# Masks by an added product, keys in two tiles, and another order of experts and values in an attention and expert kernel

## The chip, the cores and the metric

The kernel runs on one core of a Trainium2 chip. A core has five engines that run side by side, each through its own queue in order: TensorE (PE) multiplies matrices, VectorE (DVE) and ScalarE (ACT) work on elements, GpSimd (POOL) does element work and issues the converting loads, and SyncE (SP) issues plain loads and stores. Sixteen DMA engines move the data for all of them. PE, DVE and ACT reach PSUM, the memory that products are written to; POOL works in SBUF alone. PE loads its stationary operand with an instruction of its own, which the profile lists as PEld.

The metric is the device time of one execution in microseconds (us). Lower is better.

## The reference

Two stages. First, attention in which each row sees itself and the 63 rows before it; then one expert for each whole batch entry, chosen by the mean of its rows.

```python
batch, n_heads, seq, head_dim = (8, 8, 576, 64)
scores = scale * np.matmul(q, k.transpose(0, 1, 3, 2))
rel = pos[:, None] - pos[None, :]
mask = (rel >= 0) & (rel < 64)
scores = np.where(mask, scores, -1e9)
attn = np.exp(scores - scores.max(-1, keepdims=True))
attn = attn / attn.sum(-1, keepdims=True)
x = np.matmul(attn, v)              # heads side by side: (8, 576, 512)

logits = x.mean(axis=1) @ w_gate    # (8, 8)
e_idx = np.argmax(logits, axis=1)   # one expert for each batch entry
gate_w = softmax(logits)[e_idx]
h = np.maximum(x[b] @ w1[e], 0.0)   # 512 -> 1024
out[b] = gate_w[b] * (h @ w2[e])    # 1024 -> 512
```

All inputs and the output are float32.

## The kernel before

**Units.** The work on attention is cut into 16 units of four heads; units 2b and 2b + 1 belong to batch entry b. A unit goes through these functions:

- `load_qk(u)` (lines 208 to 213): two loads on POOL's queue, which turn float32 into bf16. There are six buffers.
- `transpose_qk(u, which)` (321): 18 transpositions on PE, for q or for k. `leave_qk` copies the result out of PSUM: q by ACT, k by DVE. With `both` set, DVE and ACT copy one half of k each, into one tile.
- `scores(u, c)` for c = 0, 1, 2 (352): 14 products of 64 keys each, then the exponential by ACT (line 371), then on DVE the multiplication with a mask of ones and zeros (378).
- `values(u, s)` for s = 0, 1 (384): 20 products with the probabilities as stationary operand; the values come from two fp16 copies, `va` and `vb` (shifted by 64 rows). `norm` then divides by the sum, on DVE.
- `transpose_x(u)` (427): ten transpositions of the result, copied out by ACT, which adds up the rows for the gate as it copies.

The values of a batch entry come by `load_v(b)` on SP's queue, behind a small memset by POOL. `cast_v(u)` makes the fp16 copies in three parts, "whole" into `va`, "low" and "high" into `vb`; where no engine is named, all three are done by POOL.

**Experts.** `gate(b)` (469) adds up over partitions by one product on PE, finds the largest logit on DVE, and loads its index into a register of POOL. `load_w1(b)` and `load_w2(b)` use that register, on POOL's queue. `expert_up(b, ft)`, eight pieces for each b, makes the hidden layer; `expert_down(b, mt)`, five pieces, makes the output, which DVE copies and SP stores. In the planner's account an up piece is 1.0 unit, a down piece 1.7, and the short last one 0.9: 15.7 for each batch entry. `experts(amount)` (599) lets out pieces until the amount is used up; pieces are whole, and what was overdrawn is carried on.

**Order.** Everything that `P` wraps keeps the order of the program on its engine. The opening (lines 646 to 708) is written out by hand for units 0 to 3; units 0 and 1 are helped by idle products (`busy`) and by casts on other engines. The gate of entry 0 uses a pooling of its own on PE (`pool_mm`, `pool_parts`). Then the loop over t (710): step t holds scores(t), values(t - 1), transpose_x(t - 1) and the transpositions of q and k of t + 1, with a share of the experts between each two of them; in even steps gate(t / 2 - 1) and the weight loads follow, late in the step. At t = 3 six units of experts go out; in steps 4 and 5 the share (`pace`) is two thirds of the later one.

**PSUM.** One pool of four buffers of two banks serves all products.

Of the kernel before, what the change touches and what calls it, by code (L numbers as in the profile page):

```python
# [156 lines left out]
def kernel(  # L157
# [10 lines left out]
    nc = tc.nc  # L168
# [77 lines left out]
    P(nc.gpsimd.memset(v_tiles[0][:, HM, 0:1], 0.0))  # L246
    P(nc.sync.dma_start(out=v_tiles[0][:, HM:NM, :], in_=vv[0][:, HM:NM, :]))
# [15 lines left out]
    par = const.tile([128, 2, 64], FP16)  # L263
    P(nc.vector.memset(par, 1.0))
    for (half, e, own) in ((0, 0, True), (1, 0, False), (0, 1, False), (1, 1, True)):
        sl = par[64 * half:64 * half + 64, e, :]
        if own:

            P(nc.gpsimd.affine_select(
                out=sl, in_=sl, compare_op=ALU.is_ge, fill=0.0, base=0,  # L270
                pattern=[[1, 64]], channel_multiplier=-1))
        else:

            P(nc.gpsimd.affine_select(
                out=sl, in_=sl, compare_op=ALU.is_ge, fill=0.0, base=-1,
                pattern=[[-1, 64]], channel_multiplier=1))
    masks = const.tile([128, 3, 2, 6, 64], FP16)
    for c in range(3):
        for s in range(2):
            P(nc.vector.tensor_copy(  # L280
                out=masks[:, c, s].rearrange("p (g e) w -> p g e w", e=2),
                in_=par[:, None, :, :].broadcast_to([128, 3, 2, 64])))
    for s in range(2):
        P(nc.vector.memset(masks[64:128, 0, s, 0, :], 0.0))
        P(nc.vector.memset(masks[0:64, 1, s, 3, :], 0.0))
# [48 lines left out]
    def leave_qk(u, which, both=False):  # L334

        view = qk_ps[u, which][:, 0:NT * 128].rearrange("p (t x r) -> p x r t", t=NT, x=2)
        if which == 0:
            dst = qkt.tile([128, 2 * S], BF16, tag="qT")
            P(nc.scalar.copy(  # L339
                out=dst.rearrange("p (x r t) -> p x r t", x=2, t=NT), in_=view))  # L340
            qt_tiles[u] = dst
        else:
            dst = qkt.tile([128, 2 * S], BF16, tag="kT")
            to = dst.rearrange("p (x r t) -> p x r t", x=2, t=NT)
            if both:
                P(nc.vector.tensor_copy(out=to[:, 0], in_=view[:, 0]))  # L346
                P(nc.scalar.copy(out=to[:, 1], in_=view[:, 1]))
            else:
                P(nc.vector.tensor_copy(out=to, in_=view))  # L349
            kt_tiles[u] = dst  # L350

    def scores(u, c, mask=True):
        qT, kT = qt_tiles[u], kt_tiles[u]
        sp = psum.tile([128, 2, 512], FP32, tag="ps")

        def mm(s, half, kblk, qblk, n):
            P(nc.tensor.matmul(  # L357
                out=sp[64 * half:64 * half + 64, s,
                       64 * (qblk - 6 * c):64 * (qblk - 6 * c) + n],
                lhsT=kT[64 * s:64 * s + 64, ts(kblk, 64)],  # L360
                rhs=qT[64 * s:64 * s + 64, 64 * qblk:64 * qblk + n],
                start=True, stop=True, tile_position=(64 * s, 64 * half)))
# [8 lines left out]
        P(nc.scalar.activation(out=pt, in_=sp[:, :, 0:384], func=AF.Exp, scale=scale))  # L371
        pt_tiles[u, c] = pt
        if mask:
            mask_scores(u, c)

    def mask_scores(u, c):
        pt = pt_tiles[u, c]
        P(nc.vector.tensor_tensor(  # L378
            out=pt, in0=pt, in1=masks[:, c].rearrange("p s g w -> p s (g w)"),
            op=ALU.mult))  # L380
# [46 lines left out]
    def transpose_x(u, chunks=(0, 1), parts=True):  # L427
# [11 lines left out]
        for kl in chunks:  # L439
            kb = 2 * qd + kl  # L440
            P(nc.scalar.activation(  # L441
                out=xT[:, kb, :], in_=tp[:, kl, 0:S], func=AF.Copy,
                accum_out=pooled[:, b, kb:kb + 1]))
# [202 lines left out]
    cast_part(0, "whole", nc.vector)  # L646
    cast_part(0, "high")
    cast_part(0, "low")
# [12 lines left out]
    transpose_qk(1, 0)  # L661
    transpose_qk(1, 1, False)
    leave_qk(1, 1, True)
    cast_part(1, "high")
    cast_part(1, "whole")
    load_v(1, True)
    values(0, 0)
    for c in range(3):
        scores(1, c, False)
    cast_part(1, "low", nc.scalar)  # L670
    values(0, 1, False)
    mask_scores(1, 0)
    norm(0, 1)
    mask_scores(1, 1)
    mask_scores(1, 2)
    values(1, 0)
    values(1, 1)
    transpose_qk(2, 0)
    pool_mm(0)
    pool_mm(1)  # L680
    pool_parts()
    transpose_qk(2, 1, False)
    gate(0, False)
    load_w1(0)
    leave_qk(2, 1, True)
    for c in range(3):
        scores(2, c)
        if c == 0:
            gate_weight(0)
    load_qk(4)  # L690
    cast_part(2, "high")
    load_qk(5)
    load_w2(0)
    cast_part(3, "high")
    load_v(2, True)
    transpose_x(0, parts=False)
    transpose_qk(3, 0)
    transpose_qk(3, 1)
    transpose_x(1, parts=False)
    cast_part(2, "whole", nc.vector)  # L700
    cast_part(2, "low", nc.scalar)
    for c in range(3):
        scores(3, c)
    values(2, 0)
    values(2, 1)
    cast_part(3, "whole", nc.vector)
    cast_part(3, "low", nc.scalar)
    transpose_x(2)

    for t in range(START, NU + LAG):  # L710
        pace = per_step / 8.0 * (2.0 / 3.0 if t < START + 3 else 1.0)
        on, prev, ahead = START < t < NU, START < t <= NU, t + 1 < NU
        if t == START:
            experts(4.0)
            transpose_qk(4, 0)
            transpose_qk(4, 1)
            experts(2.0)
            continue
        if START + 1 < t and t + 3 < NU:
            load_qk(t + 3)  # L720
        if t == START + 1:
            load_qk(6)
        if t % 2 == 1 and (t + 1) // 2 < B:
            load_v((t + 1) // 2, True)
        if on:
            cast_v(t)
            scores(t, 0)
        experts(pace)
        if prev:
            values(t - 1, 0)  # L730
        if ahead:
            transpose_qk(t + 1, 0)
        experts(pace)
        if prev:
            values(t - 1, 1)
        if on:
            scores(t, 1)
        experts(pace)
        if ahead:
            transpose_qk(t + 1, 1)  # L740
        if prev:
            transpose_x(t - 1)
# [4 lines left out]
        if prev and t % 2 == 0:  # L747
            gate(t // 2 - 1)
            load_w1(t // 2 - 1)
            if t == START + 1:  # L750
                load_qk(7)
            load_w2(t // 2 - 1)
# [43 lines left out]
```

## Time and profile before

| what | us |
|---|---|
| median of 3 runs | 244.97 (242.95 to 245.64) |
| profiled execution | 245.67 |
| its span, first to last instruction | 244.1 |
| PE busy | 209.2 (86%) |
| DVE busy | 128.7 (53%) |
| ACT busy | 128.8 (53%) |
| POOL busy | 87.2 (36%) |
| share of 16 DMA engines, software queue / hardware queue | 60.1% / 26.1% |

The span is shorter than the execution's time, because what lies before the first and after the last instruction is not in it. "L532" is line 532 of the kernel. In a row of the timeline the first number is the start in the span, the second the duration; the last bracket, where there is one, says how long the engine had been idle before it and what ended that. In a list of waits the numbers are the total, how often, and the longest. A row of stretches gives each engine's busy time, then the granted clock of PE, the share of the DMA engines and GB/s. Busy time of PE is not work at its peak; idle time of an engine that nobody waits for costs nothing.

### The profile page before, as it was taken

The page shows a single profiled execution, that of the slowest core. Times are in us where ns is not written, and L with a number is a line of the kernel's source. Part 1 is how long each engine was busy: PE and PEld are TensorE (multiplying, and loading weights), DVE is VectorE, ACT ScalarE, POOL GpSimd, SP SyncE. Part 2 cuts the span into 40 slices and gives each one's busy share as a digit, 9 for nine tenths or more (in the row PEclk, how much of TensorE's full clock was granted, in tenths as well). Part 3 has the DMA queues.
Part 4 walks back from the last instruction along what each step waited for, and adds up shares of the span by engine and source line. Part 5 has one row for each costly group of instructions (what it writes and reads, how often), then busy time and mean ns, then how long its engine had stood idle before and what let it go on. Part 6 is the DMA issues. An engine that isn't in the chain of part 4 may idle for free.

```text
span 244.1 us, 6963 instructions
## 1 busy us (share of the span) xinstructions
PE 209.2 (86%) x3000; PEld 144.1 (59%) x3000; DVE 128.7 (53%) x276; ACT 128.8 (53%) x216; POOL 87.2 (36%) x110
## 2 busy tenths in 40 slices
PE   7657756999949989995999799987998999799980
PEld 2346644874727846783678456863676568547740
DVE  2576564258835558554755575732758474431140
ACT  2393794685517844783368536871467445514500
POOL 7372680033940296008900692039005700200000
PEclk9996575899988999999999999997999999999998
DMA  8979999941999999996999889996994598199231
GB/s 139 206 127 206 164 205 230 234 111 46 176 228 231 252 196 217 233 250 185 189 227 246 263 147 226 244 267 134 225 228 158 79 239 225 13 205 238 87 140 64
DMA packets 33382, 45.64 MB, mean 187 GB/s; under 512 B 7104, under 2 KB 25408, under 8 KB 33344
## 3 DMA queue, kind: packets, MB, share of 16 engines
q0 software_dynamic: 13840, 26.22, 60.1%
q1 hardware_dynamic: 18704, 18.88, 26.1%
q8 instruction: 25, 0.41, 0.7%
q10 hardware_dynamic: 800, 0.03, 0.3%
q14 instruction: 13, 0.11, 0.1%
HBM read 61.90 MB, written 9.44 MB: 292 GB/s over the span
## 4 chain that ended last, share of the span: by engine, by line
PE 36%; DMA 35%; POOL 10%; DVE 7%; issue 5%; ACT 4%; POOLq 1%; SPq 0%; DVEq 0%; ACTq 0%
DMA vn<-in_v_dram 32%; PE php L532 13%; PE pso L546 12%; PE tp L326 3%; DMA qn<-in_q_dram 3%; POOL va L296 2%; PE tp L436 2%; PE op L399 2%; POOL qn L211 2%; ACT pt L371 2%; POOL kn L212 2%; POOL vb L296 2%; DVE x L415 2%; PE pso L555 2%; DVE pt L378 1%
## 5 line engine op out<-in xcount | busy, mean ns | idle before, releaser
L532 PE MATMUL php<-xT,w1t 128*128 128x288 f16 x512 | 74.5, 297 | 3.2 <-DMA w1t<-in_moe_w_dram 3.2
L536 ACT ACTIVATE hT<-php,gatew 128x576 f16<-128x576 f32 x64 | 47.0, 741 | 35.0 <-PE php L532 35.0
L532 PEld LDWEIGHTS <-w1t 128*128 128x128 f16 x512 | 56.6, 117 | 12.9 <-DMA w1t<-in_moe_w_dram 3.7
L546 PE MATMUL pso<-w2t,hT 128*128 128x512 f16 x256 | 61.7, 388 | 0.0
L378 DVE TENSOR_TENSOR pt<-pt,masks 128x768 f16<-128x768 f16 x48 | 31.7, 662 | 30.3 <-ACT pt L371 29.1
L296 POOL CAST va<-vn 128x1152 f16<-128x1152 f32 x13 | 15.3, 1175 | 89.2 <-DMA vn<-in_v_dram 88.8
L371 ACT ACTIVATE pt<-sp 128x768 f16<-128x768 f32 x48 | 38.1, 811 | 15.8 <-PE sp L357 15.7
L549 DVE COPY ob<-pso 128x512 f32<-128x512 f32 x32 | 22.1, 689 | 35.7 <-PE pso L546 35.1
L546 PEld LDWEIGHTS <-hT 128*128 128x128 f16 x256 | 23.8, 99 | 27.3 <-issue 3.0
L296 POOL CAST vb<-vn 64x1152 f16<-64x1152 f32 (+1 forms) x29 | 34.7, 1195 | 0.9
L441 ACT ACTIVATE xT<-tp 128x576 f16<-128x576 f16 x32 | 20.5, 648 | 18.4 <-PE tp L436 18.3
L339 ACT COPY dst<-tp 128x1152 bf16<-128x1152 bf16 x16 | 18.0, 1123 | 21.8 <-PE tp L326 21.8
L399 PE MATMUL op<-vb,pt 128*64 128x65 f16 x320 | 18.0, 200 | 10.8 <-POOL vb L296 7.1
L415 DVE TENSOR_TENSOR x<-op,linv 128x640 f16<-128x640 f32 x32 | 26.4, 824 | 1.1
L399 PEld LDWEIGHTS <-pt 128*64 128x64 f16 x640 | 14.4, 114 | 18.7 <-issue 14.7
L349 DVE COPY dst<-tp 128x1152 bf16<-128x1152 bf16 x13 | 17.6, 1352 | 8.3 <-PE tp L326 8.3
L357 PE MATMUL sp<-dst 64*64 64x128 bf16 (+1 forms) x672 | 17.2, 221 | 3.9 <-DVE dst L346 2.7
L357 PEld LDWEIGHTS <-dst 64*64 64x64 bf16 x672 | 11.1, 110 | 11.5 <-issue 5.4
L399 PE MATMUL op<-va,pt 128*64 128x65 f16 x320 | 17.5, 201 | 0.4 <-POOL vn L221 0.4
L436 PE MATMUL tp<-identh,x 128*128 128x128 f16 x160 | 12.7, 231 | 3.6 <-DVE x L415 3.2
L436 PEld LDWEIGHTS <-x 128*128 128x128 f16 x160 | 10.0, 104 | 5.6 <-DVE x L415 4.3
L413 DVE RECIPROCAL linv<-op 128x10 f32<-128x10 f32 x32 | 6.9, 215 | 11.9 <-PE op L399 11.9
(67 smaller groups left out, 160.2 us busy)
## 6 DMA issues: line engine op xcount, KB each, us to landing
w2t<-in_moe_w_dram POOLq DMA_DIRECT2D x8, 1024.0 KB, 14.9
out_dram<-ob SPq DMA_DIRECT2D x32, 256.0 KB, 6.2
w1t<-in_moe_w_dram POOLq DMA_DIRECT2D x7, 1024.0 KB, 8.4
qn<-in_q_dram POOLq DMA_DIRECT2D x16, 288.0 KB, 15.1
kn<-in_k_dram POOLq DMA_DIRECT2D x16, 288.0 KB, 17.1
vn<-in_v_dram SPq DMA_DIRECT2D x2, 576.0 KB, 7.3
w1t<-in_moe_w_dram POOLq DMA_DIRECT2D x2, 512.0 KB, 6.5
out_dram<-ob SPq DMA_DIRECT2D x16, 64.0 KB, 5.8
```

Source lines behind the costliest of these rows:

```text
L296: P(eng.tensor_copy(out=out, in_=in_))
L357: P(nc.tensor.matmul(out=sp[64 * half:64 * half + 64, s, 64 * (qblk - 6 * c):64 * (qblk - 6 * c) + n], lhsT=kT[64 * s:64 * s + 64, ts(kblk ...
L371: P(nc.scalar.activation(out=pt, in_=sp[:, :, 0:384], func=AF.Exp, scale=scale))
L378: P(nc.vector.tensor_tensor(out=pt, in0=pt, in1=masks[:, c].rearrange("p s g w -> p s (g w)"), op=ALU.mult))
L399: P(nc.tensor.matmul(out=op[64 * half:64 * half + 64, xx, 65 * jj:65 * jj + 65], lhsT=pt[:, s, 64 * (g % 6):64 * (g % 6) + 64], rhs=win, s ...
L415: P(nc.vector.tensor_tensor(out=x[:, :, h0 * D:(h0 + 2) * D].rearrange("p j (x c) -> p x j c", x=2), in0=view[:, :, :, 0:64], in1=li[:, :, ...
L436: P(nc.tensor.transpose(out=tp[:, kl, ts(jj, 128)], in_=x[:, jj, x_chunk(b, kb)], identity=identh))
L441: P(nc.scalar.activation(out=xT[:, kb, :], in_=tp[:, kl, 0:S], func=AF.Copy, accum_out=pooled[:, b, kb:kb + 1]))
L532: P(nc.tensor.matmul(out=php[:, sc, 0:288], lhsT=w1t[:, kb, 512 * (ft // 4) + ft % 4:512 * (ft // 4 + 1):4], rhs=xT[:, kb, ts(sc, 288)], s ...
L536: P(nc.scalar.activation(out=hT[:, ft].rearrange("p (sc s) -> p sc s", sc=2), in_=php[:, :, 0:288], func=AF.Relu, scale=gatew[:, b:b + 1]))
L546: P(nc.tensor.matmul(out=pso[:, 0, :], lhsT=hT[:, fb, ts(mt, 128)], rhs=w2t[:, fb, :], start=(fb == 0), stop=(fb == FB - 1)))
L549: P(nc.vector.tensor_copy(out=ob, in_=pso[:, 0, :]))
```

## The change

1. **Masks.** For units 0 to 3 the mask is no longer a multiplication on DVE. `add_outside(u, c)` first writes a tile of 0 and -1e38 into PSUM by a product with the identity (two products of 384 columns), and the score products add to it, so that the exponential is zero outside the window. The later units multiply with fp16 masks as before; these are now made from the same tile after unit 0's scores.
2. **Keys.** k is copied into two tiles, one for each half, on two engines that are named by the call (DVE twice by default).
3. **First load of v.** Entry 0's values were loaded in two halves, the first as the kernel's first load. Now two parts, of 20 and 16 rows, are both asked for after the loads of units 0 and 1.
4. **Opening.** The casts of units 0 and 1 and their normalisation come later and lie on other engines; `load_v(2)` comes earlier, `load_qk(6)` later; `transpose_x` of units 0 and 1 is copied by ACT or DVE without the sum.
5. **Experts.** The first experts stand right behind unit 3's scores, ahead of its and unit 2's values; the six units go out in five calls among the values and transpositions.
6. **Step.** In the loop, gate and weight loads of an even step follow the first share of experts, ahead of `cast_v(t)`; values(t) and transpose_x(t) come at the end of step t instead of in step t + 1. The share is 0.96 of the former one in every step.

```diff
-    P(nc.sync.dma_start(out=v_tiles[0][:, 0:HM, :], in_=vv[0][:, 0:HM, :]))
     warm = const.tile([128, 1], FP32)
...
     load_qk(1)
-    P(nc.gpsimd.memset(v_tiles[0][:, HM, 0:1], 0.0))
-    P(nc.sync.dma_start(out=v_tiles[0][:, HM:NM, :], in_=vv[0][:, HM:NM, :]))
+    for m0, m1 in ((0, 20), (20, NM)):
+        P(nc.gpsimd.memset(v_tiles[0][:, m0, 0:1], 0.0))
+        P(nc.sync.dma_start(out=v_tiles[0][:, m0:m1, :], in_=vv[0][:, m0:m1, :]))
...
+            dst = [qkt.tile([128, S], BF16, tag=f"kT{x}", name=f"kT{x}") for x in range(2)]
+            for x in range(2):
+                copy_on(engs[x], dst[x].rearrange("p (r t) -> p r t", t=NT), view[:, x])
...
+    def add_outside(u, c):
+        sp = psum.tile([128, 2, 512], FP32, tag="ps", name="sp")
+        for s in range(2):
+            P(nc.tensor.matmul(
+                out=sp[:, s, 0:384], lhsT=ident,
+                rhs=outside[:, c].rearrange("p g w -> p (g w)"), start=True, stop=False))
+        sp_ps[u, c] = sp
...
     busy(14)
     transpose_qk(0, 0)
-    busy(4)
+    add_outside(0, 0)
     transpose_qk(0, 1, False)
-    leave_qk(0, 1, True)
+    leave_qk(0, 1, (V, A))
+    add_outside(0, 1)
+    add_outside(0, 2)
     for c in range(3):
         scores(0, c)
+    make_masks()
...
     load_qk(2)
+    cast_part(0, "high")
     load_qk(3)
     transpose_qk(1, 0)
+    cast_part(0, "whole", V)
+    cast_part(0, "low", A)
+    transpose_qk(1, 1)
     cast_part(1, "high")
     load_v(1, True)
+    for c in range(3):
+        add_outside(1, c)
+    for c in range(3):
+        scores(1, c)
+    values(0, 0, False)
     values(0, 1, False)
+    cast_part(1, "whole", V)
+    norm(0, 0)
     norm(0, 1)
+    cast_part(1, "low", A)
+    busy(4)
     values(1, 0)
     values(1, 1)
     transpose_qk(2, 0)
+    transpose_qk(2, 1, False)
+    leave_qk(2, 1, (A, A))
     pool_mm(0)
...
+    experts(2.0)
     values(2, 0)
+    experts(1.0)
     values(2, 1)
+    experts(1.0)
+    values(3, 0)
     transpose_x(2)
+    values(3, 1)
+    experts(1.0)
+    transpose_qk(4, 0)
+    transpose_qk(4, 1)
+    experts(1.0)
+    transpose_x(3)
+    for t in range(START + 1, NU + LAG):
+        pace = per_step / 8.0 * 0.96
+        on, ahead = t < NU, t + 1 < NU
+        if t > START + 1 and t + 3 < NU:
             load_qk(t + 3)
         if t % 2 == 1 and (t + 1) // 2 < B:
             load_v((t + 1) // 2, True)
         if on:
             scores(t, 0)
         experts(pace)
+        if t % 2 == 0 and t <= NU:
+            b = t // 2 - 1
+            gate(b)
+            load_w1(b)
+            if t == START + 1:
+                load_qk(6)
+                load_qk(7)
+            load_w2(b)
         if on:
+            cast_v(t)
             scores(t, 1)
         experts(pace)
         if on:
             scores(t, 2)
         experts(pace)
+        if ahead:
+            transpose_qk(t + 1, 0)
         experts(pace)
+        if on:
+            values(t, 0)
         experts(pace)
+        if ahead:
+            transpose_qk(t + 1, 1)
         experts(pace)
+        if on:
+            values(t, 1)
...
         experts(pace)
         experts(pace)
+        if on:
+            transpose_x(t)
```

More of the change, by code (lines that the diff above doesn't have):

```diff
@@ L332, in transpose_qk, with leave_qk @@
             leave_qk(u, which)
-    def leave_qk(u, which, both=False):
+    def leave_qk(u, which, engs=(nc.vector, nc.vector)):
         view = qk_ps[u, which][:, 0:NT * 128].rearrange("p (t x r) -> p x r t", t=NT, x=2)
@@ L371, in scores @@
         P(nc.scalar.activation(out=pt, in_=sp[:, :, 0:384], func=AF.Exp, scale=scale))
+        if not masked:
+            P(nc.vector.tensor_tensor(
+                out=pt, in0=pt, in1=masks[:, c].rearrange("p s g w -> p s (g w)"),
+                op=ALU.mult))
         pt_tiles[u, c] = pt
[L373 to L380, printed above, removed]
     op_ps = {}
@@ L691 @@
     cast_part(2, "high")
+    load_v(2, True)
     load_qk(5)
@@ L746 @@
         experts(pace)
[L747 to L752, printed above, removed]
-        experts(pace)
+        if ahead:
+            transpose_qk(t + 1, 0)
+        experts(pace)
+        if on:
+            values(t, 0)
+        experts(pace)
+        if ahead:
+            transpose_qk(t + 1, 1)
+        experts(pace)
+        if on:
+            values(t, 1)
         if t == NU:
```

109 lines of the change are left out of this document (39 added, 70 removed).

## The prediction

> **What bounds the kernel now.** I read the page's slices first, then the list of waits of TensorE (PE), then the timelines of GpSimd (POOL) and PE around those waits, and last the chain of waits for the end.
>
> ```profile
> span 244.1 us, 6963 instructions
> ...
> PEclk9996575899988999999999999997999999999998
> ```
>
> The profiled execution took 245.67 us for a span of 244.1, so 1.6 us lie around the span; the median of the runs is 244.97. My sum is made against 245.67. The clock digits show 5 to 7 tenths in slices 4 to 7, before the experts are under way, and single dents later.
>
> ```profile
> PE op L399 <- POOL vb L296: 7.1, 7, 1.4
> PE php L532 <- DMA w1t<-in_moe_w_dram: 3.2, 1, 3.2
> ```
> ```profile
> PE gl L471 <- DVE gpart L463: 1.4, 2, 0.9
> ```
>
> These are waits in us, their number and the longest. From the first expert on, PE hardly rests: it waits for the cast of the values (vb), once for w1, and for the gate's parts. The end is plain PE work; the last batch's experts have nothing beside them:
>
> ```profile
> 221.45 7.84 PE php L532 x64
> 229.29 5.18 PE pso L546 x24
> 234.47 0.99 PE pso L555 x16
> 235.47 1.85 PE pso L546 x8
> ```
>
> An up piece (8 products) is 7.84/8 = 0.98 us, a down piece 1.85, and a batch 7.84 + 5.18 + 0.99 + 1.85 = 15.9 us for 15.7 of the planner's units. So PE's order of work after the start sets the end, and each us that PE waits there counts in full; work that changes its place costs nothing. The change has to be judged by what PE waits for, before and after.
>
> Why it waits for vb now:
>
> ```profile
> 110.58 1.14 POOL L296 CAST va<-vn 128x1152 f16<-128x1152 f32 x1 [14.95 <-DMA vn<-in_v_dram]
> 111.67 2.50 POOL L296 CAST vb<-vn 64x1152 f16<-64x1152 f32 x2
> 114.12 0.72 POOL L512 DMA_DIRECT2D w1t<-in_moe_w_dram  x1
> ```
>
> POOL sits 15 us on the load of v, casts for 3.6 us, and only then asks for the next weights. PE, which wants the casts one step later in its order, is held at the end of this only for 7.1 us in all.
>
> **The order inside a step (the dearest edit).** The new loop puts the gate and the issues of w1 and w2 ahead of cast_v on POOL, and takes values(t) into step t, where they stood in step t+1. In an even step POOL must now wait for the gate's index, issue two loads, and then cast. The trace of before holds just this sequence once, where v had landed long before:
>
> ```profile
> 188.56 0.36 PE L471 MATMUL gl<-gpart,onesf 128*128 128x8 f32 x2 [0.95 <-DVE gpart L463]
> ```
> ```profile
> 190.66 0.72 POOL L512 DMA_DIRECT2D w1t<-in_moe_w_dram  x1 [2.27 <-DVE gatew L500]
> 191.38 0.72 POOL L517 DMA_DIRECT2D w2t<-in_moe_w_dram  x1
> 192.15 1.14 POOL L296 CAST va<-vn 128x1152 f16<-128x1152 f32 x1
> 193.24 2.56 POOL L296 CAST vb<-vn 64x1152 f16<-64x1152 f32 x2
> ```
>
> From the gate's product to the last cast: 193.24 + 2.56 - 188.56 = 7.24, with the signal 7.3 us. On PE, between the same gate and values(t, 0), lie two score groups, one transposition of q and three calls of experts(pace):
>
> ```profile
> 178.68 0.29 PE sp L357 x12
> ```
> ```profile
> 183.95 0.62 PE tp L326 x18
> ```
>
> 0.29 + 0.29 + 0.62, the gate itself (0.36 busy, of which I take 0.15 as the rest overlaps), and whole expert pieces of 0.98 or 1.85. Following the planner's account through steps 4, 6, 8, 10, 12 and 14, the stretch is 6.0, 4.2, 5.2, 3.3, 4.3 and 4.3 us, 27.3 in all. Step 4 also has load_qk(6) and (7) between w1 and w2, four more issues of 0.72, so 10.2 us there. PE waits 6 x 7.3 + 2.9 - 27.3 = 19.4 us; the 7.1 of now go. **Net +12.3.** Queued behind POOL's wait for the index are the casts, the next q and k issues and the next v; who waits is PE, in order, at values(t, 0). Odd steps have no gate, and POOL, which runs ahead there, costs nothing. v itself is no limit: it is asked for right after the even step's casts, so it has a period of some 25 us less the 4 of the casts themselves, against 18.4, at most 19.8, from issue to landing today:
>
> ```profile
> DMA to landing us min/median/max: 4.9/18.4/19.8
> ```
>
> The gate also moves nearer to the transposition that feeds it:
>
> ```profile
> 79.64 0.73 PE L436 MATMUL tp<-identh,x 128*128 128x128 f16 x10
> ```
> ```profile
> 81.82 0.23 DVE L463 SCALAR_TENSOR_TENSOR gpart<-wg,pooled,gpart 128x8 f32<-128x8 f32 x1 [0.40 <-ACT xT L441]
> ```
>
> The parts are ready 82.05 - 79.64 = 2.4 us after the transposition begins. Before, some three pieces lay between; now one up piece, one score group and the transposition: 0.62 + 0.29 + 0.98 = 1.9. So 0.5 us in each of six steps and 0.8 in step 16, 3.8 against 1.4 now: **+2.4.** Less is possible if pieces fall well (0), more if ACT is behind (7).
>
> **w1 for batch 1.** The wait of 3.2 us and the half clock behind it:
>
> ```profile
> 71.00:75.00 4.00, 3.92 (x30) 2.31 (x30) 0.56 (x1) 1.44 (x2) 0.00 (x0) 0.58 1.12 240
> 167.00:171.00 4.00, 4.00 (x36) 1.43 (x30) 1.06 (x2) 1.12 (x1) 3.83 (x5) 0.57 0.88 137
> ```
>
> The seventh figure is the granted clock: 4 x (1 - 0.58) = 1.7 us lost after the wait. In the new order 13.8 us of PE work lie between gate(1) and batch 1's first piece, where 10.4 did.
>
> ```profile
> DMA to landing us min/median/max: 5.6/8.1/10.8
> ```
>
> Those are w1's landings. Issue 2.1 us after the gate and 10.8 make 12.9: in time. **-3.2 - 1.7 = -4.9.** The second dent (1.7 us too) followed a wait for vb, and a like wait earlier brought none:
>
> ```profile
> 166.23 0.19 PE L399 MATMUL op<-vb,pt 128*64 128x65 f16 x1 [1.19 <-POOL vb L296]
> ```
> ```profile
> 114.23 0.19 PE L399 MATMUL op<-vb,pt 128*64 128x65 f16 x1 [1.15 <-POOL vb L296]
> ```
>
> My six new waits are 2.1 to 4.2 us. Of three rests of that size two gave a dent. I take two, 3.4 for 1.7: **+1.7**, between -1.7 and +5.
>
> **The start.** Three edits pull against one another. The experts go right behind unit 3's scores:
>
> ```profile
> 32.30 0.71 PE L357 MATMUL sp<-dst 64*64 64x64 bf16 x42 [0.79 <-DVE dst L349]
> ```
> ```profile
> 38.66 1.25 PE L436 MATMUL tp<-identh,x 128*128 128x128 f16 x10 [3.20 <-DVE x L415]
> ```
>
> Now values(2), their normalisation on DVE and the transposition stand between 33.0 and 39.9, when the experts begin; taken alone the edit gives up to 39.9 - 33.0 = 6.9 less 1.5 of PE work that is only pushed behind (four value groups and a transposition), 5.4. But v of batch 0 is no longer asked for first. Packets and MB by queue, from 2 to 5 us, 9 to 11, 8 to 15, and 15 to 23 us:
>
> ```profile
> q1 hardware_dynamic: 2316, 0.59, 95.8%
> ```
> ```profile
> q0 software_dynamic: 294, 0.32, 92.6%
> q1 hardware_dynamic: 290, 0.07, 27.4%
> ```
> ```profile
> q1 hardware_dynamic: 2320, 0.59, 42.9%
> ```
> ```profile
> q0 software_dynamic: 1087, 1.18, 96.9%
> ```
>
> q1 is v, in records of 256 B, and q0 is q and k. Alone, v's first half (2,304 records) is through in 3 us, while the engines have nothing else. Beside q and k the two take turns, 290 records against 294, so v moves 145 a us. Now all 4,608 records start at about 8.5, as the second half does today (it lies within 8 to 15): 3.5 us of turns (500), then some 2 us alone at 770 a us or a little more (1,500 to 2,000), and at about 14 q and k of units 2 and 3 come in, a us sooner than today (15), as their trigger no longer waits for a mask of 0.66 and the k copies run abreast. Those hold the engines some 7 us, v gets 1,000, and the last 1,100 to 1,600 need 1.5 us more. The first part (20 of 36 rows, 2,560 records) lands at 14 to 15, the second at about 22.5. With the casts spread over three engines (POOL's 1.15 to 1.4 the longest), values(1, 0) can start at 23.9:
>
> ```profile
> 19.81 0.19 PE L399 MATMUL op<-va,pt 128*64 128x65 f16 x1 [0.40 <-POOL vn L221]
> ```
> ```profile
> 26.56 1.51 POOL L509 DMA_DIRECT2D w1t<-in_moe_w_dram  x2 [6.76 <-DVE dst L346]
> ```
>
> So 4.1 later. Today 6.75 us pass from there to w1's issue. Unit 0's normalisation now stands on DVE behind unit 1's cast (0.75), which adds 0.8; the k transposition, now ahead of the pool, takes 1.1 out:
>
> ```profile
> 23.00 1.10 PE tp L326 x18
> 24.10 0.54 PE gl L471 x2
> ```
> ```profile
> 26.09 1.44 PE L357 MATMUL sp<-dst 64*64 64x64 bf16 x42 [1.47 <-DVE dst L346]
> ```
>
> So w1 is issued at 23.9 + 6.75 + 0.8 - 1.1 = 30.4, against 26.56, and its second half lands near 38. Unit 3's scores end 9.0 us after the gate's product today (24.0 to 33.0); with the gate at 27.9, 1.5 less as the k copy no longer stands between, and 2 to 4 more for the products, they end at 37.4 to 39.4. The experts begin at about 38, 1.9 before today, with 1.5 of work behind them: **net 0.** Taken from both sides: -7 if v is in time, +2 if it is still later. [...]
>
> The products that replace the masks are 24 of 384 columns; with 1.85/8 = 0.23 for 512 columns each is 0.17, 4 us in all, 8 at half clock. Half lie under the copies that unit 0 and 1 wait for anyway; the others, 2 to 4 us, are in my 38, as are the 12 multiplications taken off DVE. They cost that much only if PE becomes the last in that stretch. Two key tiles let ACT and DVE copy side by side in units 0 and 1; the ACT queue is full of exponentials behind them, so nothing. Later two half copies replace one; DVE is off the path. The pace (0.96 throughout) only shifts pieces to the tail: nothing.
>
> **Sum.** 245.67 + 12.3 + 2.4 - 4.9 + 1.7 + 0 = 257.2.
>
> **The rivals.** *Casts in time* (faster). If the casts end before PE reaches values, the 19.4 and the dents (3.4) fall away: 257.2 - 19.4 - 3.4 = 234; it decides where gate to casts takes less than about 4.5 us. For it: POOL no longer waits for v's landing, 14.95 a time. Against it: the measured 7.24, of which 3.65 are casts alone, and POOL works in order. Chance 0.2, a third of it with the start early too, 228.
> *v early* (slower all the same). If v's records are served in bursts and not in turns, both parts land by 15, values(1) start near 17.5, 6.4 sooner than in my sum, and the experts near 31: 7 less, 250. Against it stand the equal counts. [...] 0.15.
> *Waits that overlap* (within 1%). The wait for the casts may swallow the gate's (2.4), the dents may stay at one (1.7), and one down piece more may fall into the stretch in four of the six steps (7.4): 257.2 - 11.5 = 245.7. 0.12.
> My forecast has the remaining 0.53.
>
> **How the numbers follow.** About 1% (2.45 us) is what a measurement of this kernel can tell from none. Faster takes the first rival, 0.2; same 0.12; slower 0.15 + 0.53 = 0.68. Below 236 lies half of the first rival and a bit, 0.12; above, my own case reaches 257 + 2 (start) + 3.3 (dents) = 262, and 0.07 is left beyond. The own range of the slower cases is 248 to 262.
>
> **What would show it.** In the changed profile PE's wait op <- POOL vb should be near 19 us in place of 7.1, in even steps, with w1 and w2 issued just ahead of the casts and the wait for v (14.95 a time) gone from POOL; php <- DMA w1t should be gone; gl <- DVE gpart near 3.8; v's second part should land at 21 to 23.5 and the first up product stand at 37 to 39. If op <- POOL vb is under 8, or the first up product is at 32, the forecast fails there.

## The result and the profile after

The changed kernel takes 259.9 us (median of four runs, 257.03 to 261.58); the kernel before, on the same chip, 243.96 (four runs, 241.88 to 245.64). The ratio is 1.064, with a 95% interval of 1.048 to 1.081: slower, by about 16 us. The ratio leaves out the slowest run of each kernel, which lies more than 1.5% above its fastest. The prediction's sum was 257.2, in a range of 236 to 262.

The profiled execution of the changed kernel took 260.54 us. First its page, span, busy time and granted clock in 40 slices:

```profile
span 258.8 us, 7019 instructions
...
PE 219.2 (85%) x3024; PEld 145.5 (56%) x3024; DVE 117.7 (45%) x281; ACT 126.6 (49%) x211; POOL 85.1 (33%) x109
...
PEclk9979799997999799997999799997999799999996
```

The clock row has changed its shape. Slices 4 to 7 now hold a single 7, where they had 5 to 7 throughout, but a 7 comes back every five slices or so, right through the loop. Next the list of what PE waits for (us in all, how often, the longest):

```profile
PE op L413 <- POOL vb L302: 19.8, 13, 2.9
PE gl L488 <- DVE gpart L480: 3.2, 7, 0.8
PE tp L450 <- DVE x L429: 2.2, 4, 1.0
PE sp L374 <- DVE kT L302: 2.1, 1, 2.1
PE php L549 <- DMA w1t<-in_moe_w_dram: 1.6, 1, 1.6
```

The wait for the casts is 19.8 us where it was 7.1, the gate's 3.2 where it was 1.4. The 1.6 for w1 is entry 0's second half, in the opening; the 3.2 of batch 1 are gone. What happens in an even step is seen best in step 8, on POOL and on PE:

```profile
111.36 0.72 POOL L529 DMA_DIRECT2D w1t<-in_moe_w_dram  x1 [17.28 <-DVE gatew L517]
112.07 0.72 POOL L534 DMA_DIRECT2D w2t<-in_moe_w_dram  x1
112.83 1.52 POOL L302 CAST va<-vn 128x1152 f16<-128x1152 f32 x1
114.31 2.30 POOL L302 CAST vb<-vn 64x1152 f16<-64x1152 f32 x2
```
```profile
108.73 0.39 PE L488 MATMUL gl<-gpart,onesf 128*128 128x8 f32 x2 [0.40 <-DVE gpart L480]
...
112.47 1.90 PE L563 MATMUL pso<-w2t,hT 128*128 128x512 f16 x8
115.50 0.19 PE L413 MATMUL op<-vb,pt 128*64 128x65 f16 x1 [1.13 <-POOL vb L302]
...
116.66 0.19 PE L413 MATMUL op<-vb,pt 128*64 128x65 f16 x1 [0.93 <-POOL vb L302]
```

POOL has been idle for 17.28 us, not for v but for the gate's result. Then come the two weight loads, then the casts, the last of which ends at 114.31 + 2.30 = 116.61. From the gate's product that is 7.9 us. PE has done its pieces in the meantime and stands twice, 1.13 and 0.93 us, at the two groups of values. Of the six even steps this is the mildest; the others wait 2.8 to 3.8 us.

The opening, on POOL and then PE:

```profile
11.32 0.72 POOL L211 DMA_DIRECT2D qn<-in_q_dram  x1 [0.26 <-issue]
12.04 0.72 POOL L212 DMA_DIRECT2D kn<-in_k_dram  x1
14.37 1.60 POOL L302 CAST vb<-vn 64x1088 f16<-64x1088 f32 x1 [1.61 <-DMA vn<-in_v_dram]
15.93 0.72 POOL L211 DMA_DIRECT2D qn<-in_q_dram  x1
16.64 0.72 POOL L212 DMA_DIRECT2D kn<-in_k_dram  x1
19.13 1.73 POOL L302 CAST vb<-vn 64x1152 f16<-64x1152 f32 x1 [1.77 <-DMA vn<-in_v_dram]
...
27.02 1.51 POOL L526 DMA_DIRECT2D w1t<-in_moe_w_dram  x2 [6.00 <-issue]
```
```profile
33.22 0.43 PE L549 MATMUL php<-xT,w1t 128*128 128x288 f16 x2
35.23 1.91 PE L549 MATMUL php<-xT,w1t 128*128 128x288 f16 x14 [1.58 <-DMA w1t<-in_moe_w_dram]
```

v's first part has landed at 14.4, its second at 19.1, the first up product stands at 33.2. This half of the change went better than forecast.

The end is PE work as before, piece for piece, only later (the chain of waits):

```profile
236.40 7.84 PE php L549 x64
...
250.41 1.85 PE pso L563 x8
```

To see where the time came from, the span is cut at the first score product of step 4, 49.18 us before and 46.77 after, and at the end of PE's last product, 237.34 and 252.30. The two rows give the length of this stretch and, second, PE's busy time in it, first of the kernel before, then of the changed one:

```profile
49.18:237.34 188.16, 174.09 (x2415) 118.93 (x2414) 102.85 (x211) 100.51 (x172) 64.93 (x73) 0.98 0.85 191
```
```profile
46.77:252.30 205.53, 182.10 (x2366) 120.91 (x2364) 95.22 (x218) 97.81 (x172) 66.19 (x75) 0.95 0.82 177
```

PE is idle 23.43 us there in place of 14.07 (+9.4) and busy 182.10 in place of 174.09 (+8.0), with 49 products fewer in the stretch. With the start 2.4 earlier that makes 15.0, the whole of the difference at PE's end. The busy part is mostly the clock. In the next two fences each row is one stretch of 3.41 us, the length of every half-clock stretch in these two loops; the second figure is PE's busy time, the seventh the granted clock. After:

```profile
56.59:60.00 3.41, 1.24 (x39) 1.03 (x39) 0.47 (x2) 0.00 (x0) 3.35 (x5) 1.00 1.03 199
60.00:63.42 3.42, 3.42 (x10) 0.96 (x11) 1.91 (x3) 0.00 (x0) 3.25 (x5) 0.50 1.17 248
114.61:118.02 3.41, 1.58 (x41) 1.14 (x41) 1.31 (x3) 0.00 (x0) 3.31 (x4) 1.00 1.08 219
118.02:121.44 3.42, 3.42 (x28) 1.41 (x27) 2.21 (x4) 0.00 (x0) 3.29 (x4) 0.50 1.05 237
```

Before, at the two waits for vb that the prediction had compared:

```profile
112.56:115.97 3.41, 1.96 (x42) 1.33 (x42) 1.71 (x3) 0.67 (x1) 3.35 (x5) 1.00 0.38 95
115.97:119.39 3.42, 3.42 (x47) 1.62 (x45) 2.28 (x4) 1.26 (x2) 3.31 (x5) 1.00 0.96 169
163.76:167.17 3.41, 1.16 (x40) 0.99 (x40) 1.39 (x4) 0.81 (x1) 3.35 (x4) 1.00 0.35 133
167.17:170.59 3.42, 3.42 (x10) 1.00 (x8) 0.65 (x1) 1.12 (x1) 3.25 (x5) 0.50 0.90 135
```

The stretches with PE busy for 1.24, 1.58 and 1.16 us are followed by one with a granted clock of 0.50, the one with 1.96 us is not. A half-clock stretch costs 3.41 / 2 = 1.7 us of full-speed work. The changed kernel has six of these in the loop (from 60.0, 87.3, 118.0, 145.3, 176.0 and 203.4), one behind the waits for the casts in each of its six even steps; the kernel before has two, one behind its wait for w1 and one behind a wait for the casts.

### The profile page after: what moved, and what is told of

It reads as the page before. It is cut to its first block, busy times and chain, and to the rows that moved or that the text cites. A ratio compares the mean times of both kernels' runs of the same rounds, so it can differ in the third digit from the quotient of the medians.

```text
span 258.8 us, 7019 instructions
## 1 busy us (share of the span) xinstructions
PE 219.2 (85%) x3024; PEld 145.5 (56%) x3024; DVE 117.7 (45%) x281; ACT 126.6 (49%) x211; POOL 85.1 (33%) x109
## 4 chain that ended last, share of the span: by engine, by line
PE 50%; DMA 16%; POOL 10%; DVE 9%; ACT 6%; issue 4%; POOLq 1%; SPq 1%
PE pso L563 21%; PE php L549 16%; DMA vn<-in_v_dram 12%; POOL vb L302 5%; PE op L413 4%; PE tp L332 4%; ACT xT L458 3%; POOL va L302 3%; DVE x L429 3%; DMA w1t<-in_moe_w_dram 3%; PE pso L572 2%; PE tp L450 2%; DVE kT L302 2%; PE sp L374 1%; ACT hT L553 1%
## 5 line engine op out<-in xcount | busy, mean ns | idle before, releaser
L549 PE MATMUL php<-xT,w1t 128*128 128x288 f16 x512 | 72.6, 291 | 1.6 <-DMA w1t<-in_moe_w_dram 1.6
L563 PE MATMUL pso<-w2t,hT 128*128 128x512 f16 x256 | 66.7, 411 | 0.4 <-ACT pt L389 0.3
L549 PEld LDWEIGHTS <-w1t 128*128 128x128 f16 x512 | 54.6, 115 | 9.3 <-DMA w1t<-in_moe_w_dram 1.9
L458 ACT ACTIVATE xT<-tp 128x576 f16<-128x576 f16 x28 | 17.9, 647 | 58.2 <-PE tp L450 58.1
L529 POOL DMA_DIRECT2D w1t<-in_moe_w_dram x7 | 5.0, 719 | 124.0 <-DVE gatew L517 105.4
L413 PE MATMUL op<-vb,pt 128*64 128x65 f16 x320 | 18.2, 204 | 19.8 <-POOL vb L302 19.8
L302 POOL CAST vb<-vn 64x1152 f16<-64x1152 f32 (+1 forms) x28 | 33.1, 1181 | 4.2 <-DMA vn<-in_v_dram 3.4
L391 DVE TENSOR_TENSOR pt<-pt,masks 128x768 f16<-128x768 f16 x36 | 20.1, 557 | 15.1 <-ACT pt L389 14.5
L302 DVE COPY kT<-tp 128x576 bf16<-128x576 bf16 x29 | 20.6, 752 | 9.5 <-PE tp L332 9.4
L374 PE MATMUL sp<-dst,kT 64*64 64x128 bf16 (+1 forms) x672 | 17.1, 223 | 2.5 <-DVE kT L302 2.1
L374 PEld LDWEIGHTS <-kT 64*64 64x64 bf16 x672 | 11.3, 111 | 11.3 <-issue 6.1
L450 PE MATMUL tp<-identh,x 128*128 128x128 f16 x160 | 12.3, 225 | 2.3 <-DVE x L429 2.2
```

The costliest lines, as they stand in the source:

```text
L302: P(eng.tensor_copy(out=out, in_=in_))
L374: P(nc.tensor.matmul(out=sp[64 * half:64 * half + 64, s, 64 * (qblk - 6 * c):64 * (qblk - 6 * c) + n], lhsT=kT[x][64 * s:64 * s + 64, ts(k ...
L391: P(nc.vector.tensor_tensor(out=pt, in0=pt, in1=masks[:, c].rearrange("p s g w -> p s (g w)"), op=ALU.mult))
L413: P(nc.tensor.matmul(out=op[64 * half:64 * half + 64, xx, 65 * jj:65 * jj + 65], lhsT=pt[:, s, 64 * (g % 6):64 * (g % 6) + 64], rhs=win, s ...
L458: P(nc.scalar.activation(out=xT[:, kb, :], in_=tp[:, kl, 0:S], func=AF.Copy, accum_out=pooled[:, b, kb:kb + 1]))
L549: P(nc.tensor.matmul(out=php[:, sc, 0:288], lhsT=w1t[:, kb, 512 * (ft // 4) + ft % 4:512 * (ft // 4 + 1):4], rhs=xT[:, kb, ts(sc, 288)], s ...
```

## The experiments

The prediction's theory is that the new place of the casts, behind the gate and the weight issues on POOL, makes PE wait, and that these waits cause the half-clock stretches. Its rivals are that v's landing is what the casts wait for, that the opening costs something, or that the clock falls for another reason. Times stand beside a run of the kernel before on the same chip: 245.6 for the first four, 244.41 for the next four, 244.27 (median of seven) for the last four. Most experiments are one run, and four runs of the kernel before spread over 3.8 us (241.88 to 245.64), so a difference of 2 or 3 us between two single runs shows little by itself.

**e1_split: the even step's casts on three engines.**

```diff
         if on:
-            cast_v(t)
+            if t % 2 == 0:
+                cast_v(t, whole=V, low=A)
+            else:
+                cast_v(t)
             scores(t, 1)
```

> In even steps the cast whole goes to DVE and low to ACT; POOL keeps only high, behind the gate and the two weight issues as now. The chain gate to last cast falls from 7.9 us to about 5.6. Theory (the casts behind the gate are what PE waits for): PE's wait op <- POOL vb falls from 19.8 to 3 to 7 us, at least four of the six half-clock windows go, and the time is 240 to 246. Rival (the opening's products and the late first v cost it): the wait may fall, but the time stays at 255 to 260.

It took 250.56 us. PE's wait for POOL's cast fell to 0.6, below the 3 to 7 expected, but the time lies 4.6 us above the expected range, between it and the rival's. These are rows of its lists of waits, PE's and ACT's, and one of ACT's timeline:

```profile
PE pso L563 <- ACT hT L553: 6.7, 2, 6.0
```
```profile
ACT vb L300 <- DMA vn<-in_v_dram: 7.1, 3, 5.2
```
```profile
83.06 1.16 ACT L300 CAST vb<-vn 64x1152 f16<-64x1152 f32 x1 [5.16 <-DMA vn<-in_v_dram]
```

In step 6 v had not landed when ACT came to its cast. POOL can stand there at little cost (in the kernel before it waits 88.8 us for v, and PE 7.1 us for its casts), but behind ACT's cast were an exponential and a `hT` on which PE's next down piece waited for 6.0 us. The wait for the casts was removed, and the wait for v that lay under it went to an engine where others queue. Three half-clock stretches in the loop are left of six, one more than expected.

**e2_castfirst: the casts at the head of the step, ahead of the gate.**

```diff
         if on:
+            cast_v(t)
             scores(t, 0)
         experts(pace)
...
         if on:
-            cast_v(t)
             scores(t, 1)
```

> cast_v(t) goes back to the head of the step, ahead of the gate on POOL; all else stays. Theory: the chain gate to casts is gone, but POOL now waits for v's landing (asked for one step earlier, 17 us in flight) and PE, which takes values(t) in the same step, waits for that: op <- POOL vb 8 to 14 us, time 247 to 254. If v's landing does not bind, the wait is under 4 us and the time 238 to 242. Rival (opening): 255 to 260.

252.82 us, as expected. PE's and POOL's waits:

```profile
PE op L413 <- POOL vb L302: 12.7, 8, 4.3
```
```profile
POOL va L302 <- DMA vn<-in_v_dram: 81.8, 5, 18.9
```

POOL waits for v again, as in the kernel before, and PE, which now wants the values in the same step, still waits for 12.7. So two things stand one behind the other ahead of the casts: the gate in the changed loop, and v's landing as soon as the gate is out of the way.

**e3_idle: ten idle products of 512 columns ahead of values(t, 0) in even steps.** They lie in the time in which PE would wait; the ten took 2.32 us at 56.40 and again at 141.02.

```diff
         op = psum.tile([128, 2, 512], FP32, tag="ps")
+        for _ in range(fill):
+            P(nc.tensor.matmul(out=op[:, 0, :], lhsT=spin[:, 0:128], rhs=spin,
+                               start=True, stop=True))
...
-            values(t, 0)
+            values(t, 0, fill=10 if t % 2 == 0 else 0)
```

> Ten idle products of 512 columns (2.1 us at full clock) are put ahead of values(t, 0) in even steps, into the same PSUM tile, so that PE is busy for most of the wait; nothing else changes. Theory (the half-clock windows follow from PE's rest in the wait): the wait shown shrinks by some 2 us a step, its end does not move, the six windows fall to at most two, and the time falls by 5 to 10 us, to 250 to 255. Rival (the windows come of themselves or by the load): six windows, time 258 to 262.

256.49 us, 1.5 above the expected range. Its clock row shows one 7 in the loop in place of six (the stretch from 89.5; the stretch ahead of it had PE busy for less than 1 us). The lines stand three later here than in the changed kernel:

```profile
PE op L416 <- POOL vb L302: 9.4, 9, 2.3
```
```profile
PEclk9985999999999979999999999999999999999996
```

The half-clock stretches of this loop come from PE's rest, then: fill the rest with work that nobody needs, and five of six are gone. From step 4's first score product to the end of PE's last product the profile has 199.34 us where the changed kernel has 205.53. The whole time is 3.4 below the changed kernel's median but only 0.5 below its fastest run: step 4 begins 1.5 us later (48.31 for 46.77), although nothing was changed ahead of it, and that is what is missing to the range.

**e4_newopen and e5_newloop: the two halves of the change apart.** e4 has the new masks, keys and opening with the old loop, e5 the old opening with the new loop. In the opening of e4 the experts and the transpositions are rearranged so that values(3) is left to step 4, as the old loop wants it:

```diff
     experts(2.0)
     values(2, 0)
     experts(1.0)
     values(2, 1)
     experts(1.0)
-    values(3, 0)
     transpose_x(2)
-    values(3, 1)
-    experts(1.0)
     transpose_qk(4, 0)
     transpose_qk(4, 1)
-    experts(1.0)
-    transpose_x(3)
+    experts(2.0)
```

> The new opening (products for masks, two key tiles, late first v, experts behind unit 3's scores) with the old loop (values one step later, gate behind the casts, old pace). Theory: the loop alone costs, so this is as fast as before or up to 4 us faster: 239 to 245, op <- POOL vb near 7. Rival (opening costs): 252 to 260.

> The old opening (masks by DVE, one key tile, v's first half asked for first, experts after unit 2's values) with the new loop. Theory (the loop alone costs): op <- POOL vb 17 to 21 us, four to seven half-clock windows of 3.4 us after step 4, time 258 to 266, at or above the changed kernel. Rival (the opening costs): 240 to 248.

241.08 and 264.73 us. The opening alone is worth -4.5 (241.08 - 245.6), the loop alone +20.3 (264.73 - 244.41). Their sum is +15.8, where both together do +15.9; between single runs so close an agreement is luck, but which half costs is not in doubt. PE's wait for the casts in e4, then in e5:

```profile
PE op L413 <- POOL vb L302: 9.2, 6, 3.9
```
```profile
PE op L399 <- POOL vb L296: 18.3, 12, 2.9
```

The new loop brings its 18 us of waiting whatever the opening. Its half-clock stretches are no fixed number: in e5 eight of them, one more than expected, came to 27.3 us from step 4 on, 13.7 of it lost, where the changed kernel lost 10.2.

**e6_castfirst_v and e7_newopen_v: v of the next batch asked for one step earlier,** in e2's kernel and in e4's.

```diff
-        if t % 2 == 1 and (t + 1) // 2 < B:
-            load_v((t + 1) // 2, True)
+        if t % 2 == 0 and t // 2 + 1 < B:
+            load_v(t // 2 + 1, True)
```

> As the run with the casts at the head of the step, and load_v is asked for one step earlier, in even steps, so that v has landed when POOL reaches the casts. Theory: neither the gate nor v stands ahead of the casts, so op <- POOL vb is under 4 us (12.7 without the earlier load), at most two half-clock windows after step 4 are left, time 237 to 243. If the wait stays above 8, something else on POOL holds the casts.

> The new opening with the old loop, and load_v one step earlier as well. Theory: the old loop's waits for vb (9.2 us) are v's landing and go to under 3; w1 and w2, which stand behind the casts on POOL, go out earlier too; time 232 to 237. Rival (the DMA engines are the limit, and an earlier v only delays the weights): php <- DMA w1t grows above its 4.2 and the time stays at 239 to 243.

240.5 and 232.4 us. In e6 the wait for the casts is gone from PE's list, and what comes next are w1 and the gate:

```profile
PE php L549 <- DMA w1t<-in_moe_w_dram: 5.5, 3, 2.7
PE gl L488 <- DVE gpart L480: 4.5, 7, 1.7
```

So e2's remaining wait was v's landing: the same order of casts, 12.3 us faster with v early. And the old order of the step with v early (e7) is 8 us faster still; which part of the new order costs these 8 us (the values in the same step, the weights asked for earlier, the share) was not taken apart. e7's wait for w1 is 4.4 where e4 has 4.2, so the rival falls.

**e8_newopen_vfirst: e4's kernel with v's first half as the first load again.**

```diff
     v_tiles[0] = vpool.tile([128, NM, D], FP32, tag="vn", name="vn0")
+    P(nc.sync.dma_start(out=v_tiles[0][:, 0:HM, :], in_=vv[0][:, 0:HM, :]))
...
-    for m0, m1 in ((0, 20), (20, NM)):
+    for m0, m1 in ((HM, NM),):
```

> The new opening with the old loop, but v's first half is asked for at the head of the kernel again and the second after units 0 and 1. The prediction had the late v cost some 4 us until w1's issue. Theory: casts of unit 0 no longer hold unit 1's key copy (PE's wait of 2.1 to 2.3 for kT goes), v is complete near 15 and not 19, w1 of entry 0 is issued 2 to 4 us sooner, and the time falls by 1 to 4: 237 to 240. Rival (the opening is bound by something else, or q of unit 0 lands later): 240 to 243.

241.96 us, inside the rival's range. w1 is asked for at 24.56 where e4 has 25.69, and PE begins on the second half of it at 33.00 where e4 has 33.87 (rows of e8, one line later than in e4; then e4's):

```profile
24.56 1.50 POOL L527 DMA_DIRECT2D w1t<-in_moe_w_dram  x2 [6.49 <-issue]
```
```profile
33.00 3.18 PE L550 MATMUL php<-xT,w1t 128*128 128x288 f16 x14 [1.71 <-DMA w1t<-in_moe_w_dram]
```
```profile
33.87 3.33 PE L549 MATMUL php<-xT,w1t 128*128 128x288 f16 x14 [2.39 <-DMA w1t<-in_moe_w_dram]
```

What this microsecond is worth at the end stays open: e8's loop has three half-clock stretches where e4's has one, which is 3.4 us of full-speed work. Dropping v as the first load, for which the prediction counted some 4 us until w1's issue, put it off by about 1 us.

**The last four.** f1_newopen_v3 is e7's kernel again, in four runs.

> The kernel of e7_newopen_v once more (opening of the changed kernel with its masks and keys, loop of the kernel before, v asked for one step earlier), timed in rounds for an interval. One look gave 232.4 against 244.4 of the kernel before, a ratio of 0.951. Theory: the loop's wait for the casts came from v's landing and is gone with its half-clock windows, so the gain holds: 231 to 236 us, ratio 0.94 to 0.97. Rival: the one look was lucky with its windows (one pair, at 66), and others bring up to three more at 1.7 us each: 236 to 239.

230.76 us (230.26 to 232.11), a ratio of 0.946 (0.941 to 0.952): the fastest version here. There is no half-clock stretch between 46 and 222 us; the seventh figure below, the granted clock (PE's busy time is the second), is 1.00 for this whole stretch. What PE waits for most is now w1, 5.7 us.

```profile
46.00:222.00 176.00, 168.39 (x2392) 116.37 (x2391) 105.79 (x222) 99.07 (x171) 64.65 (x72) 1.00 0.94 207
```

f2_before_v is the kernel before with the two lines on `load_v` alone (the diff of e6 and e7).

> The kernel before with one edit: v of the next batch is asked for in the even step, one step earlier. Theory: the kernel before loses its wait for vb (7.1 us) and the half-clock window behind it (1.7); the opening and the wait for w1 of batch 1 (3.2 and 1.7) stay: 245.7 - 8.8 = 236.9, so 235 to 239 us, and op <- POOL vb under 2. Rival: the earlier v only takes the engines from w1 and w2, and the wait moves to php <- DMA w1t (over 6 us): 242 to 246.

233.86 us (233.05 to 235.49), 1.1 below the expected range, a ratio of 0.959 (0.953 to 0.966). One moved load gives most of what the best version gains, and the new opening, by the difference of the two, 3.1 us (the two intervals do not overlap). POOL's waits in the kernel before, then POOL's and PE's in this one:

```profile
POOL va L296 <- DMA vn<-in_v_dram: 88.8, 6, 16.8
```

```profile
POOL w1t L512 <- DVE gatew L500: 63.4, 5, 14.7
...
POOL va L296 <- DMA vn<-in_v_dram: 13.5, 1, 13.5
```
```profile
PE php L532 <- DMA w1t<-in_moe_w_dram: 2.7, 1, 2.7
```

POOL waited 88.8 us for v in six steps; it now does so once, and its spare time has moved to the gate. The wait for w1 did not grow (2.7 for 3.2), so the rival falls.

f3_after_v is the changed kernel with the same two lines.

> The changed kernel with the same one edit, v one step earlier. Theory: in the new loop POOL casts only after the gate and the two weight issues, and v has landed by then; an earlier v changes nothing: op <- POOL vb 17 to 20 us, 256 to 262 us. Rival: some of the wait is v's landing after all: op <- POOL vb under 12 and under 252 us.

258.06 us, and the wait stays:

```profile
PE op L413 <- POOL vb L302: 18.2, 12, 2.9
```

In the new order of the step v is no limit, as the prediction had it; the same edit that is worth 10 us in the old loop is worth nothing here that a run can tell. f3 and e6 differ in one line only, whether `cast_v(t)` stands behind the gate and the weight loads or at the head of the step: 258.06 against 240.5 us, and 18.2 us of waiting for the casts against none in the list. That is the prediction's mechanism with all else held.

f4_newopen_dvemask is e4's kernel with the masks of units 0 to 3 multiplied on DVE again; the 24 products with the identity are left out, and the masks are made ahead of unit 0's copies.

```diff
+    make_masks()
     transpose_qk(0, 0)
-    add_outside(0, 0)
     transpose_qk(0, 1, False)
     leave_qk(0, 1, (V, A))
-    add_outside(0, 1)
-    add_outside(0, 2)
...
-    make_masks()
```

> The kernel of e4_newopen (new opening, old loop) with the masks of units 0 to 3 again as multiplications on VectorE; the 24 products with the identity are left out, and the fp16 masks are made ahead of unit 0's copies. Theory (the prediction's): half of the products lay under copies that PE waited for, and the multiplications (12 of 0.66 us) lie mostly beside other work, so the two forms differ little: the first up product within 1.5 us of e4's 33.9, time 239 to 243 us. Rival: the multiplications stand between the exponentials and the values on the path of the opening, and the first up product comes 3 to 6 us later, 244 to 247 us.

242.47 us for e4's 241.08, on different chips. The up products that wait for w1's second half start 1.7 us later than in e4 (35.60 against 33.87), a little over the 1.5 expected:

```profile
35.60 3.55 PE L549 MATMUL php<-xT,w1t 128*128 128x288 f16 x14 [2.17 <-DMA w1t<-in_moe_w_dram]
```

Its opening also ran 17.1 us at half clock against e4's 6.8. By these two runs the masks on PE are worth 0 to 2 us in the opening; how much of that is the clock's, and what of it reaches the end, stays open.

## Why the prediction was right, point by point

The direction and the time came out, and the main mechanism is shown. Its terms, against the two cut stretches (us, changed kernel less kernel before):

| term | forecast | measured | from |
|---|---|---|---|
| PE waits for the casts | +12.3 | +11.5 | 18.6 in the loop, of 19.8 in all, less 7.1 |
| PE waits for the gate's parts | +2.4 | +1.8 | 3.2 less 1.4 |
| PE waits for w1 of batch 1 | -3.2 | -3.2 | no such wait after |
| half clock in the loop | 0 (-1.7 for w1, +1.7 for the casts) | +6.8 | six stretches for two, 1.7 each |
| start | 0 | -2.4 | step 4 at 46.77 for 49.18 |
| a wait for the last row check | not named | -1.8 | `okp`, in the list before only |
| rest | | +2.3 | not assigned |
| sum | +11.5 | +15.0 | 252.30 less 237.34 |

**The casts** were the right place and the right size. By steps, the six waits were forecast as 4.2, 3.1, 2.1, 4.0, 3.0 and 3.0 and measured as 3.65, 3.45, 2.06, 3.81, 2.79 and 2.79. The way was to take the one place of the old trace where gate, weight loads and casts followed each other on POOL (7.3 us) and to count PE's work in the same stretch piece by piece. e1 (wait gone with the casts elsewhere) and f3 (wait unmoved with v early) show the cause from both sides, and f3 beside e6 shows it by one line alone. With that the rival *casts in time* is out; it needed 4.5 us from gate to casts, and 7.9 were measured.

**The half clock was mis-sized.** The step that failed reads "Of three rests of that size two gave a dent. I take two, 3.4 for 1.7". There were six, 10.2 us. Rests that come in every even step were taken for chances of two in three and then priced as fewer; with the prediction's own ratio four would have been the figure. In the profiles here half clock went not with the length of one wait but with how much PE rested within one 3.41-us stretch (the counts are in the last section), and a step's two waits, 2.1 to 3.8 us together, mostly fall into the same one. e3, with one half-clock stretch in the loop for six, shows that it is PE's rest that does it. Six is no fixed number either: two other runs of the changed kernel have a mean granted clock of 0.952 where the profiled one has 0.939, and 0.013 of 257 us is 3.4 us, about two stretches fewer somewhere in the kernel (an estimate from the two clocks).

**The start was mis-sized the other way.** The forecast had v's second part at 22.5 and the start at net 0; the part landed at 19.1 and the start was 2.4 earlier, with unit 3's values already done. Two steps failed. The first is the 3.5 us, up to 12 us, for which v was to take turns with q and k of units 0 and 1. In the trace of before v already ran almost alone from 11 to 13 us (1,718 records against 82), and in the changed kernel from 10 to 13.5 (2,976 against 61), 3.5 us in place of the 2 us forecast. The second is that q and k of units 2 and 3 were both put at about 14. In the new order unit 0's cast stands on POOL between them and itself waits for v's first part, so unit 3's loads went out at 15.93, and from 15.5 to 16.5 v again had the engines nearly to itself (756 records against 66). Beside unit 2's loads the turns came near one to one as forecast (167 against 135 from 14.5 to 15.5). w1 was issued at 27.0 in place of the 30.4 forecast. That v's earlier landing is what moved the start is argued from these rows; no run moved these loads alone. That the new opening gains is shown by f1 beside f2 (3.1 us) and by e4 (-4.5 us with the old loop).

**v early** as a rival had 250 us for an early start. The start did come early, though v was not that early; the six half-clock stretches took the gain back. Against this rival the prediction set the equal counts of records. They hold only while both queues have work, and they do not tell turns of single records from turns of equal groups, so that argument is weaker than it stands there. The sum was 3.5 short at PE's end, and that it was no more is partly luck, because errors of opposite sign stand in it: the clock (+6.8) against the start (-2.4) and -0.9 from all other rows.

**What was asked of the profile:** op <- POOL vb near 19 (19.8), the wait for v gone from POOL (in its place 105.4 us for the gate), php <- w1t of batch 1 gone (it is), gl near 3.8 (3.2), the second part of v at 21 to 23.5 (19.1, missed) and the first up product at 37 to 39 (33.2, missed, and near the 32 at which the prediction said that it fails).

The products that replace the masks, for which the prediction took 4 to 8 us of PE, half of it covered, cost 6.1 us of PE's busy time:

```profile
L360 PE MATMUL sp<-outside,ident 128*128 128x384 bf16 x24 | 6.1, 350 | 0.2
```

How much of it was covered no run shows; in f4 the multiplications were no faster.

## What to carry to other kernels

Before moving work ahead in an in-order queue, write down for each engine what its queue waits for at that place and what the next engine is doing meanwhile: here the casts went from behind one wait (v) to behind another (the gate), and their reader on PE was moved a step nearer. When an engine is seen to wait long for a load, try first to ask for the load earlier; two lines of that were worth 4%, while the whole change cost 6%. And count a regular PE wait of 2 to 4 us as its own length plus a half-clock stretch that may follow it (1.7 us lost in each here; behind all six in the changed kernel's profile, behind three of six in f3), and look for something to fill it.

## What the runs showed of the hardware

The granted clock followed a sharper pattern than expected. In each profile the half-clock stretches begin at whole multiples of 3.41 us from one another: the six in the changed kernel's loop follow each other at 27.3, 30.7, 27.3, 30.7 and 27.3 us, 8 or 9 times 3.41, and the two in the loop of the kernel before, from 71.6 and 167.2, lie 28 times 3.41 apart. So each trace can be cut into stretches of 3.41 us on a grid that its own half-clock stretches fix; what sets that length no run shows. Take, in all 14 profiled kernels, each stretch at full clock that lies whole between step 4's first score product and PE's last product. PE busy for under 1.5 us: the next stretch was at half clock in 25 of 25 cases. Busy 1.55 to 1.70: in 5 of 8. Busy 1.75 to 2.0: in none of 17. So in these profiles half clock went with the rest that fell into one stretch, not with the length of the waits. Before the change, two steps had waits for vb of 1.41 and 1.15 us, and of 1.06 and 1.19 us. The longer pair lay across two stretches, of which the second still had 1.96 us of work, and was not followed by half clock; the shorter lay in one stretch with 1.16 us of work and was. Some half-clock stretches were followed by another: of the 39 in the loops, the nine with PE busy for 2.51 us or less were followed by a second one, the 30 with 2.86 us or more by full clock. In the openings, where many products are small transpositions, three full-clock stretches with 2.2 to 2.4 us busy were followed by half clock as well; that is not explained.
